# Top-k attention and a leaky-ReLU MLP on one core: first units transposed on TensorE, and the first 256-token chunk begun pair by pair

## The chip, the cores and the metric

The kernel runs on one core of a Trainium2 chip. A core has five engines that work through their own queues in order and meet at semaphores: TensorE (PE in the profile, with PEld for its weight loads), VectorE (DVE), ScalarE (ACT), GpSimd (POOL) and SyncE (SP), which here issues the DMA transfers. PE writes its results into PSUM, eight banks of 2 KB a partition; everything else lies in SBUF or in device memory. The metric is the time of one execution in device microseconds. Five executions of the kernel before took 1484.49, 1484.82, 1487.24, 1488.46 and 1490.54 us: median 1487.24.

## The reference

Attention over 8 batches with 8 heads each, 576 tokens and head size 64, where each query keeps only its 32 largest scores; then an MLP over all 4608 tokens.

```python
scores = scale * np.matmul(q, k.transpose(0, 1, 3, 2))
kth = np.partition(scores, -top_k, axis=-1)[..., -top_k:-top_k + 1]
scores = np.where(scores >= kth, scores, -1000000000.0)
attn = np.exp(scores - np.max(scores, axis=-1, keepdims=True))
attn = attn / (np.sum(attn, axis=-1, keepdims=True) + 1e-09)
attn_out = np.matmul(attn, v)
x = attn_out.transpose(0, 2, 1, 3).reshape(B * S, H * D)     # 4608 x 512
h = x @ w_in                                                 # 512 -> 2048
out = np.maximum(0.01 * h, h) @ w_out                        # 2048 -> 512
```

Everything is in float32.

## The kernel before

**Units.** Heads are taken in pairs, since two heads of 64 fill 128 partitions: 32 pairs, four to a batch (`HP = 4`). A `Unit` is 128 query rows of one pair, both heads; the 64 tokens left over from 576 = 4 x 128 + 64 go two pairs to a unit. A batch is 18 units, the whole kernel 144. In batch 0 the units go through the tokens 0 to 127 for pairs 0 to 3 (units 0 to 3), then 128 to 255 (4 to 7), 256 to 383 (8 to 11), 384 to 511 (12 to 15), and the rest (16, 17).

**A unit's way.** PE computes the scores (L214) into two "wide" PSUM tiles and one "narrow" one, two banks each; ACT copies them to SBUF (L221). DVE finds the 32 largest in four rounds (`top_k`, L244 to L252). POOL subtracts a large number from all others (`mask`, L262, L263). ACT takes the exponent and its sum (L266), adds the small constant (`sums`, giving `ze`, L271); DVE takes the reciprocal (`rz`, L275), ACT multiplies by it (`normalize`, L278). The weights must then be transposed for the product with v. Normally this goes by DMA (`transpose`): ACT splits each 32-bit word into two halves (L287, two copies), SP writes both to device memory (`apart`, L288) and reads them back with a DMA transpose into `wT` (L290). For the units in `HURRIED` PE transposes instead (`transpose_in_haste`, L300: nine 128x128 transposes into two "wide" tiles), and ACT copies the result (`keep_transposed`, L306). Last, PE multiplies v by `wT` for a couple of units (`weigh_values`, L327) and ACT copies the result into the chunk's x (`keep_values`, L341).

**Chunks.** The MLP works on chunks of tokens, two of 128 and then seventeen of 256 (`CHUNKS`). A chunk may begin when all units of all four pairs that hold its tokens have been kept; `ready_at` lists when that is. `mlp(ch)` is a generator that issues a few matmuls at a time: for the first two chunks the first layer in `hidden_of_few` (L352, then transposes L362), for the others L378 with the activation on ACT (L384), then the second layer (L390) and the output (L397, L398). In L378 the four pairs of x are the four terms of one sum in PSUM, in `ps_ml`, which has two banks. `gT` holds the hidden values of one chunk; so chunks go one after the other.

**The order of the work** is written out by hand, the same loop for all engines, and each engine executes its part of it in order. Step s of the loop at the end issues: the top-k of unit s in four slots on DVE; the mask, exponents and sums of unit s - 1; reciprocals, normalization and transposes of unit s - 2; on even s the scores of units s + 2 and s + 3; and at MIDDLE or END of a step the values of the couple of units for which `values_at` gives this place. Between the slots `mlp_steps(budget)` is called seven times. While one of the two first chunks is the latest, or none, the budget of a call is `EARLY_SHARE`; later it is the backlog divided evenly over the slots until the next chunk is ready. At the end of each step `load_more` issues loads of q, k and v of later pairs on SP.

```python
    HURRIED = (15, 23, 31)
    UNHURRIED = 14
        if n < UNHURRIED:
            return (n | 1) + LAG + 1, MIDDLE
        return (n | 1) + LAG - ((n | 1) in HURRIED), END
```

So the values of units 2 and 3 come at the middle of step 7, those of 6 and 7 at the middle of step 11, those of 14 and 15 at the end of step 17. `late` decides whether a unit's reciprocals come after the first slot of a step or after the second (`weights_of`). Before all this, until about 70 us, the weights of the MLP are loaded and put together from double words (`round_weights`).

Of the kernel before, what the change touches and what calls it, by code (L numbers as in the profile page):

```python
# [19 lines left out]
def kernel(  # L20
# [168 lines left out]
    for b in range(B):  # L189
        first = b % 2 == 1  # L190
        whole = [Unit(b, [b * HP + hp], q0 + LEFT * first)
                 for q0 in range(0, S - LEFT, P) for hp in range(HP)]
        left = [Unit(b, [b * HP + hp, b * HP + hp + 1], 0 if first else S - LEFT)
                for hp in range(0, HP, 2)]
        units += left + whole if first else whole + left
# [27 lines left out]
    def first_scores(u):  # L223

        ps = [ps_sc.tile([P, 2, 512], F32, name="wide", bufs=2) for i in range(2)]
        for half in range(2):
            for i, pi, side, r0 in u.parts:
                qt, kt = qk_of[pi]
                d = slice(side * D, (side + 1) * D)
                nc.tensor.matmul(ps[i][:, half, 0:HS], qt[d, u.q0:u.q0 + P],  # L230
                                 kt[d, half * HS:(half + 1) * HS], start=True, stop=True)
        u.both = work.tile([P, 2, S], F32, name="s_sb", bufs=5)
        u.s = [u.both[:, i, :] for i in range(2)]
        for i in range(2):
            nc.scalar.copy(u.s[i].rearrange("p (h n) -> p h n", h=2), ps[i][:, :, 0:HS])
# [129 lines left out]

    def mlp(ch):
# [6 lines left out]
        for f0 in range(0, NFC if ch >= EARLY else 0, 2):  # L373
            ph = ps_ml.tile([P, 2, CHMAX], F32, name="ph", tag="ml")
            for i in range(2):
                f = f0 + i
                for c in range(HP):
                    nc.tensor.matmul(  # L378
                        ph[:, i, 0:n], w_in[c][:, f * P:(f + 1) * P], x[c][:, 0:n],
                        start=(c == 0), stop=(c == HP - 1),  # L380
                    )
                    if c == 1 or i == 0 and c == HP - 1:
                        yield 2 * max(n, 225)
            nc.scalar.activation(gT[:, f0:f0 + 2, 0:n], ph[:, :, 0:n], AF.Prelu, alpha=SLOPE)  # L384
            yield 2 * max(n, 225)
# [24 lines left out]
    def mlp_steps(budget):  # L410
        owed[0] += budget
        while owed[0] > 0:
            if running[0] is None:
                if not ready:
                    owed[0] = 0.0
                    return
                running[0] = mlp(ready.pop(0))
# [11 lines left out]
    HURRIED = (15, 23, 31)  # L429
# [3 lines left out]
    def values_at(n):  # L433

        if n < UNHURRIED:
            return (n | 1) + LAG + 1, MIDDLE
        return (n | 1) + LAG - ((n | 1) in HURRIED), END

# [13 lines left out]
    def attended(*place):  # L452
        for at, ch in ready_at:
            if at == place:
                ready.append(ch)
                backlog[0] += mlp_cost(ch)

# [8 lines left out]
    EARLY_SHARE = 500  # L466
    SLOTS = 7

    with tc.manual_schedule():
        last = {p: n for n, u in enumerate(steps) for p in u.pairs}  # L470

        def load_more(s):

            for of, load, n, lag in ((qk_of, load_qk, LOADED + 3, -2), (v_of, load_v, LOADED_V, LAG + 1)):
                while len(of) < NPAIR and (len(of) < n or last[len(of) - n] + lag <= s):
                    load(len(of))

# [26 lines left out]
        def values(*place):  # L504
# [4 lines left out]
            else:  # L509
                return  # L510
            for part in (weigh_values, keep_values):
                for n, u in enumerate(due):
                    part(u, po[:, n, :])
            attended(*place)

        for s in range(len(steps) + LAG + 1):
# [8 lines left out]

            slot()
# [4 lines left out]
            if older and not late:  # L531
                weights_of(older)
            mlp_steps(budget)
            values(s, MIDDLE)
# [3 lines left out]
            if s - 2 in HURRIED:  # L538
# [4 lines left out]
            if older:  # L543
                keep_transposed(older) if s - 2 in HURRIED else transpose(older)
# [5 lines left out]
            if old:  # L550
                exponents(old, 1)
                sums(old)
            if new and s < HURRY:
                scores(new)
            values(s, END)
# [65 lines left out]
```

## Time and profile before

| what | value |
|---|---|
| median of five executions | 1487.24 us |
| profiled execution, its own time | 1484.49 us |
| its span, first to last instruction | 1482.7 us |
| busy PE / PEld | 1394.8 us (94%) / 928.9 us (63%) |
| busy DVE | 1328.7 us (90%) |
| busy ACT / POOL | 1096.1 us / 1096.0 us (74% each) |
| mean granted PE clock | 0.979 of full speed |
| chain that ended last, by engine | PE 77%, DVE 17%, ACT 3%, DMA 2% |
| L390, second layer, 1152 records | 509.4 us |
| L378, first layer, 2176 records | 481.8 us |
| L327, values, 3200 records | 180.2 us |
| L287, split copies, 282 | 309.1 us, 1144 ns each |
| L300, transposes on PE, 27 | three units |

How to read it: a float32 matmul leaves two records, so 64 records of L378 are 32 matmuls. "Busy" of an engine is an average over the whole span; which engine sets the pace changes between the first 240 us and the rest, and is read from busy times by stretch and from the waits. A row of the view by time gives start, duration, engine, line, operation, tiles, count and in brackets the idle time before it with the instruction that ended it. The wait of an engine that isn't the bottleneck costs nothing by itself, but an engine's queue is in order: what stands behind the waiting instruction is late too.

### The profile page before, as it was taken

How to read it: one execution, taken by the hardware profiler on the slowest of the kernel's cores; microseconds unless marked ns; L12 is line 12 of the kernel's file. 1: busy time of each engine (PE TensorE's matmuls, PEld its weight loads, DVE VectorE, ACT ScalarE, POOL GpSimd, SP SyncE). 2: the span in 40 equal slices, each digit the busy share in tenths (PEclk: the TensorE clock that was granted, in tenths of full speed). 3: DMA queues.
4: the chain of work that ended last, by engine and by line, in shares of the span. 5: the costliest groups of instructions: out<-in, count | busy, mean ns of one | idle time of the engine just before them, and what ended most of it. 6: DMA issues, size and time to landing. Idle time of an engine off the chain costs nothing.

```text
span 1482.7 us, 24084 instructions
## 1 busy us (share of the span) xinstructions
PE 1394.8 (94%) x8059; PEld 928.9 (63%) x8059; DVE 1328.7 (90%) x3414; ACT 1096.1 (74%) x1979; POOL 1096.0 (74%) x742
## 2 busy tenths in 40 slices
PE   6715998999999999999999999999999999999998
PEld 2303546676666766676767666767676767676674
DVE  7999998999999999999999999999999999999600
ACT  8647886877788877787877777777777787877720
POOL 2278887788788887788878888888888888788700
PEclk9967998999999999999999999999999999999999
DMA  8824454635565465655665555556655555654510
GB/s 320 305 63 130 120 164 123 173 111 148 155 167 155 137 167 160 182 140 151 184 163 144 139 167 171 164 142 153 182 161 145 129 142 133 165 131 140 144 47 14
DMA packets 391420, 223.48 MB, mean 151 GB/s; under 512 B 336256, under 2 KB 336256, under 8 KB 389248
## 3 DMA queue, kind: packets, MB, share of 16 engines
q1 hardware_dynamic: 391296, 221.95, 53.6%
q8 instruction: 63, 1.03, 0.3%
q14 instruction: 61, 0.50, 0.1%
HBM read 46.14 MB, written 92.60 MB: 94 GB/s over the span
## 4 chain that ended last, share of the span: by engine, by line
PE 77%; DVE 17%; ACT 3%; DMA 2%; issue 1%; POOL 0%; DVEq 0%; SPq 0%; ACTq 0%
PE pz L390 29%; PE ph L378 28%; PE wide L327 10%; DVE tops L249 6%; PE wide L214 5%; DVE pairs L252 5%; PE narrow L214 3%; DVE pairs L244 2%; PE ph L352 1%; ACT split L287 1%; DMA apart<-split 1%; DVE w_out L149 1%; ACT s_sb L266 1%; ACT s_sb L278 1%; DVE w_in L149 1%
## 5 line engine op out<-in xcount | busy, mean ns | idle before, releaser
L262 POOL TENSOR_SCALAR pen<-s_sb,tops 128x576 f32<-128x576 f32 x288 | 637.4, 2213 | 217.3 <-DVE tops L249 126.2
L249 DVE MAX8 tops<-pairs 128x8 f32<-128x288 f32 (+1 forms) x1152 | 636.8, 593 | 0.0
L390 PE MATMUL pz<-w_out,gT 128*128 128x512 f32 x1152 | 509.4, 597 | 0.0
L378 PE MATMUL ph<-x,w_in 128*128 128x256 f32 x2176 | 481.8, 381 | 0.0
L252 DVE MATCH_REPLACE8 pairs<-tops,pairs 128x288 f32<-128x288 f32 (+1 forms) x864 | 460.8, 539 | 0.0
L378 PEld LDWEIGHTS ph<-x,w_in 128*128 128x128 f32 x2176 | 411.3, 190 | 77.4 <-issue 23.1
L263 POOL TENSOR_TENSOR s_sb<-s_sb,pen 128x576 f32<-128x576 f32 x288 | 406.1, 1410 | 24.1
L390 PEld LDWEIGHTS pz<-w_out,gT 128*128 128x128 f32 x1152 | 215.9, 190 | 266.3 <-issue 264.9
L287 ACT COPY split<-s_sb 128x1152 uint16<-128x1152 uint16 x282 | 309.1, 1144 | 0.0
L278 ACT ACTIVATE s_sb<-s_sb,rz 128x576 f32<-128x576 f32 x288 | 207.0, 769 | 35.3 <-DVE rz L275 35.3
L266 ACT ACTIVATE s_sb<-s_sb,nbias 128x576 f32<-128x576 f32 x288 | 220.9, 767 | 12.7 <-POOL s_sb L263 12.7
L244 DVE TENSOR_TENSOR pairs<-s_sb 128x576 f32<-128x576 f32 x288 | 213.6, 780 | 9.9
L327 PE MATMUL wide<-wT,vt 128*64 128x128 f32 (+1 forms) x3200 | 180.2, 269 | 32.6 <-ACT s_sb L221 25.0
L327 PEld LDWEIGHTS wide<-wT,vt 128*64 128x64 f32 x3200 | 162.8, 140 | 75.0 <-ACT s_sb L221 29.6
L384 ACT ACTIVATE gT<-ph 128x512 f32<-128x512 f32 x136 | 80.6, 593 | 80.8 <-PE ph L378 80.8
L341 ACT COPY x<-wide 128x128 f32<-128x128 f32 (+1 forms) x160 | 32.2, 260 | 145.7 <-PE wide L327 145.6
L221 ACT COPY s_sb<-wide 128x704 f32<-128x704 f32 x142 | 107.1, 754 | 21.1 <-PE wide L214 21.1
L214 PE MATMUL wide<-kt,qt 64*128 64x352 f32 (+1 forms) x392 | 74.7, 491 | 24.3 <-ACT s_sb L221 23.6
L275 DVE RECIPROCAL rz<-ze 128x2 f32<-128x2 f32 x144 | 22.6, 157 | 52.5 <-ACT ze L271 52.4
L221 ACT COPY s_sb<-narrow 128x448 f32<-128x448 f32 x142 | 68.7, 536 | 0.6
L397 ACT COPY o_sb<-pz 128x512 f32<-128x512 f32 x36 | 21.1, 586 | 58.4 <-PE pz L390 58.4
L252 DVE MATCH_VALUE_LOAD pairs<-tops,pairs 128x8 f32 x864 | 63.7, 74 | 0.0
(62 smaller groups left out, 622.8 us busy)
## 6 DMA issues: line engine op xcount, KB each, us to landing
apart<-split SPq DMA_DIRECT2D x282, 288.0 KB, 2.1
raw<-in_weights_dram SPq DMA_DIRECT2D x16, 1024.0 KB, 6.5
vt<-in_vk_dram SPq DMA_DIRECT2D x32, 320.0 KB, 3.5
out_dram<-o_sb SPq DMA_DIRECT2D x36, 256.0 KB, 2.0
qt<-in_qT_dram SPq DMA_DIRECT2D x20, 288.0 KB, 4.1
kt<-in_kT_dram SPq DMA_DIRECT2D x20, 288.0 KB, 4.6
raw<-in_qT_dram SPq DMA_DIRECT2D x12, 288.0 KB, 3.1
raw<-in_kT_dram SPq DMA_DIRECT2D x12, 288.0 KB, 3.5
```

The lines of the kernel that those rows point to most:

```text
L214: nc.tensor.matmul(to[r0:r0 + u.rows, i, :], qt[d, u.q0:u.q0 + u.rows], kt[d, k0:k1], start=True, stop=True)
L244: nc.vector.tensor_tensor(pairs[:, :, n, :], u.both[:, :, 0:HS], u.both[:, :, HS:S], op)
L249: nc.vector.max(out=u.tops[:, i, r, :], in_=rest[i])
L252: nc.vector.match_replace(out=rest[i], in_to_replace=u.tops[:, i, r, :], in_values=rest[i], imm_value=LOWEST)
L262: nc.gpsimd.tensor_scalar(pen, u.s[i], u.tops[:, i, ROUNDS - 1, 7:8], MASKED, ALU.is_lt, ALU.mult)
L263: nc.gpsimd.tensor_tensor(u.s[i], u.s[i], pen, ALU.add)
L266: nc.scalar.activation(u.s[i], u.s[i], AF.Exp, bias=u.nbias[:, i:i + 1], scale=SCALE, accum_out=u.z[:, i:i + 1])
L278: nc.scalar.activation(u.s[i], u.s[i], AF.Copy, bias=0.0, scale=u.rz[:, i:i + 1])
L287: nc.scalar.copy(split, pairs[:, :, h])
L327: nc.tensor.matmul(po[side * D:(side + 1) * D, o, :], vt[:, c, side, :], u.wT[:, c + side * NKC if c + 1 < NKC else c, r:r + n], start=(c ...
L378: nc.tensor.matmul(ph[:, i, 0:n], w_in[c][:, f * P:(f + 1) * P], x[c][:, 0:n], start=(c == 0), stop=(c == HP - 1),)
L390: nc.tensor.matmul(pz[0:m, 0:DMODEL], gT[:, f, r0:r0 + m], w_out[f // 4][:, f % 4, :], start=(f == 0), stop=(f == NFC - 1),)
```

## The change

- In batch 0 the last two groups of 128 tokens are taken pair by pair: units 8 and 9 are both of pair 0, 10 and 11 of pair 1, 12 and 13 of pair 2, 14 and 15 of pair 3.
- Units 0, 1, 2, 3, 7 and 14 are transposed on PE too (`HASTY`); 3 and 7 count as hurried, so that the values of 2 and 3 come at the end of step 5, and those of 6 and 7 at the end of step 9. In the step after next to a hurried unit, before step 20, its reciprocals and normalization come first of all.
- `begin_hidden` sums half of chunk 2's first layer (8 of 16 column blocks) over the pairs 0 and 1 when the values of unit 11 are kept, and over pair 2 when those of unit 13 are, into four PSUM banks: the "narrow" tile and both of `ps_ml`. `mlp(2)` then adds pair 3.
- The copies of x after values in the middle of a step go to the end of the step, unless a chunk becomes ready there or a hurried unit is two steps back.
- The scores of units 18 and 19 use `first_scores` (only "wide" tiles), since "narrow" is taken.
- `load_more` issues v ahead of q and k, and q and k of a pair 8 steps after the last unit that used the buffer (2 steps before it until now), one pair a step.
- `EARLY_SHARE` is 510 instead of 500.

```diff
+        tiles = [(0,), (P,), (2 * P, 3 * P)] if b == 0 else [(q0,) for q0 in range(0, S - LEFT, P)]
         whole = [Unit(b, [b * HP + hp], q0 + LEFT * first)
-                 for q0 in range(0, S - LEFT, P) for hp in range(HP)]
+                 for q0s in tiles for hp in range(HP) for q0 in q0s]
...
+    def begin_hidden(ch, pairs):
+        n = CHUNKS[ch]
+        x = x_of[ch]
+        if ch not in begun:
+            first = ps_sc.tile([P, 2, 512], F32, name="narrow").rearrange("p h (f n) -> p h f n", n=CHMAX)
+            begun[ch] = [first[:, 0], first[:, 1]]
+            begun[ch] += [ps_ml.tile([P, 2, CHMAX], F32, name="ph", tag="ml") for k in range(2)]
+        done = 0
+        for f in range(NFC // 2):
+            for c in pairs:
+                nc.tensor.matmul(begun[ch][f // 2][:, f % 2, 0:n], w_in[c][:, f * P:(f + 1) * P], x[c][:, 0:n],
+                                 start=(c == 0 and f % 2 == 0), stop=False)
+                done += 1
+                if done % 2 == 0:
+                    yield 2 * n
...
-            ph = ps_ml.tile([P, 2, CHMAX], F32, name="ph", tag="ml")
+            first = 0
+            if ch in begun and f0 < NFC // 2:
+                ph, first = begun[ch][f0 // 2], HP - 1
+            else:
+                ph = ps_ml.tile([P, 2, CHMAX], F32, name="ph", tag="ml")
             for i in range(2):
                 f = f0 + i
-                for c in range(HP):
+                for c in range(first, HP):
...
-    HURRIED = (15, 23, 31)
+    HURRIED = (3, 7, 15, 23, 31)
+    HASTY = (0, 1, 2, 3, 7, 14, 15, 23, 31)
...
-        if n < UNHURRIED:
-            return (n | 1) + LAG + 1, MIDDLE
-        return (n | 1) + LAG - ((n | 1) in HURRIED), END
+        if (n | 1) in HURRIED:
+            return (n | 1) + LAG - 1, END
+        return ((n | 1) + LAG + 1, MIDDLE) if n < UNHURRIED else ((n | 1) + LAG, END)
...
     def attended(*place):
         for at, ch in ready_at:
             if at == place:
-                ready.append(ch)
+                ready.append(mlp(ch))
                 backlog[0] += mlp_cost(ch)
+        for last, pairs in ((11, (0, 1)), (13, (2,))):
+            if values_at(last) == place:
+                ready.append(begin_hidden(EARLY, pairs))
...
-    EARLY_SHARE = 500
+    EARLY_SHARE = 510
...
-            for of, load, n, lag in ((qk_of, load_qk, LOADED + 3, -2), (v_of, load_v, LOADED_V, LAG + 1)):
+            for of, load, n, lag in ((v_of, load_v, LOADED_V, LAG + 1), (qk_of, load_qk, LOADED + 3, 8)):
                 while len(of) < NPAIR and (len(of) < n or last[len(of) - n] + lag <= s):
                     load(len(of))
+                    if lag > LAG + 1 and len(of) > n:
+                        break
...
+            at_first = s < HURRY and s - 2 in HURRIED
+            if at_first:
+                weights_of(older)
             slot()
...
-            if older and not late:
+            if older and not late and not at_first:
                 weights_of(older)
             mlp_steps(budget)
-            values(s, MIDDLE)
+            weighed = values(s, MIDDLE)
+            at_once = s - 2 in HURRIED or any(at == (s, MIDDLE) for at, _ in ready_at)
+            if at_once:
+                keep(weighed, s, MIDDLE)
             slot()
             if older and late:
                 weights_of(older)
-            if s - 2 in HURRIED:
+            if s - 2 in HASTY:
                 transpose_in_haste(older)
...
             if old:
                 exponents(old, 1)
                 sums(old)
+            if not at_once:
+                keep(weighed, s, MIDDLE)
             if new and s < HURRY:
-                scores(new)
-            values(s, END)
+                if s == 16:
+                    first_scores(new[0])
+                    first_scores(new[1])
+                else:
+                    scores(new)
+            keep(values(s, END), s, END)
```

`values` now only issues the matmuls and returns what is to be kept; `keep` issues the copies of x and calls `attended`. `first_scores` takes units of fewer rows too.

## The prediction

> **What bounds the kernel now.** I read the page's 40 slices first, then busy time by stage, then TensorE's waits, then the reciprocals on VectorE, because each answer says which engine to ask next.
>
> ```profile
> PE   6715998999999999999999999999999999999998
> DVE  7999998999999999999999999999999999999600
> ...
> PEclk9967998999999999999999999999999999999999
> ```
> A slice is 37 us. TensorE (PE) is full from about slice 7 to the end, VectorE (DVE) until slice 37. TensorE has free time only early, and its clock is low there.
>
> ```profile
> 74.00:137.00 63.00, 14.45 (x114) 11.36 (x112) 62.48 (x163) 35.05 (x64) 50.66 (x33) 0.62 0.34 91
> 137.00:240.50 103.50, 91.13 (x524) 50.19 (x522) 98.24 (x257) 78.84 (x149) 83.41 (x56) 0.94 0.51 145
> 240.50:1482.70 1242.20, 1236.48 (x7251) 844.88 (x7250) 1107.19 (x2882) 928.55 (x1711) 942.72 (x631) 1.00 0.53 145
> ```
> Each row gives a stretch, its length, then busy time of PE, PEld, DVE, ACT, POOL. From 240.5 us, where chunk 2's first layer begins, PE idles 5.7 us in 1242. So either chunk 2 begins earlier, or PE has less left by then, or nothing is won. The changed kernel does some of both.
>
> ```profile
> PE wide L327 <- ACT s_sb L221: 25.0, 2, 13.5
> PE wide L214 <- ACT s_sb L221: 23.6, 1, 23.6
> PE wide L327 <- DMA wT<-apart: 5.6, 1, 5.6
> ```
> (TensorE's waits from 74 to 300 us: total, times, longest.) The first two lie before 137 us: nothing is ready. The last is unit 14's transposed weights, late by DMA.
>
> But DVE is no spectator. One unit's top-k starts (L244) every 8.86 us (404.18 to 537.11 in 15 steps), while PE needs 73.8 us for eight units and a chunk (first-layer stretches begin at 692.00 and 765.79 in the chain of waits), 9.22 a unit. DVE could be only 0.36 us a unit faster, and it has lost time:
>
> ```profile
> 219.05 0.17 DVE L275 RECIPROCAL rz<-ze 128x2 f32<-128x2 f32 x1 [3.35 <-ACT ze L271]
> 251.25 0.17 DVE L275 RECIPROCAL rz<-ze 128x2 f32<-128x2 f32 x1 [3.94 <-ACT ze L271]
> 260.49 0.17 DVE L275 RECIPROCAL rz<-ze 128x2 f32<-128x2 f32 x1 [1.86 <-ACT ze L271]
> 398.25 0.17 DVE L275 RECIPROCAL rz<-ze 128x2 f32<-128x2 f32 x1 [2.81 <-ACT ze L271]
> ```
> All its waits are of this kind: 14.6 us by step 36, 10.6 of them before step 25. The cause is ScalarE's queue standing at a copy of x that waits for PE:
>
> ```profile
> 213.40 0.43 ACT L341 COPY x<-wide 128x128 f32<-128x128 f32 x2 [4.33 <-PE wide L327]
> 240.55 0.43 ACT L341 COPY x<-wide 128x128 f32<-128x128 f32 x2 [7.49 <-PE wide L327]
> ```
> And by steps 36 to 44 attention is just in time for PE:
>
> ```profile
> 412.60 1.31 PE L327 MATMUL wide<-wT,vt 128*64 128x128 f32 x20 [0.70 <-DMA wT<-apart]
> ```
> Unit 35's transpose was issued at 424.10 and takes 4.6 us, and PE uses it at 429.12; unit 39's was issued at 458.18 and is used at 462.50. So the end can move forward only as far as the smaller of two gains: PE's at chunk 3, and DVE's by step 36 to 44. After that PE's 0.36 us a unit restores slack.
>
> **The change, part by part.**
>
> *Hasty units 0, 1, 2, 3, 7, 14.* Before, a unit's way from normalized weights to wT is two splits on ACT (2.19 us), two transfers (2.1 landing, 6.27 at unit 14), a DMA transpose (4.6): 9 to 13 us. Unit 15's row of the same profile gives the new way: nine PE transposes 1.43 us, two copies on ACT 1.17. ACT saves 1.0 us a unit. PE pays 6 x 1.43 = 8.6 us, but units 0 to 3 lie in the stretch with 14.45 of 63 us busy, so only 7 and 14 count: 2.9 us. In the cold stretch forty value matmuls took 4.12 us at 115.58 and 2.33 later, so a transpose there may cost 1.43 to 2.5; I take 2.5 early, where it delays only what follows at once.
> The Trainium skill (TensorE: Matmul & The Clock Gate, Part 1) says that the array runs at half clock until about 3.4 us of sustained work, which speaks against short transposes between idle gaps; the granted 0.62 agrees. By the rule each early transpose costs 2.9 us and the start below comes 0.4 us later than I have it.
>
> *Values of units 2, 3 at step 5's end, not step 7's middle.* Step 5 starts at 113.7. Unit 3's ze is there by then (114.69 before, with 2.2 us of splits ahead of it that go). In ACT's order the copies of the scores for units 6 and 7 (2.5 us) come first: normalize to about 117. PE first runs the values of 0, 1 (cold, 4 us), then unit 3's transposes to about 121.5; copies to 122.8; values of 2, 3 (cold, 3.8) to 126.6; copy of x 0.4. The first layer of chunk 0 starts at 127 instead of 137.0: 10 us. Lower bound of the gain 5 (the two "wide" PSUM buffers are now shared with transposes and may make each other wait), upper 13 (clock warm).
>
> *What PE then has to do until chunk 2 is complete.* Chunk 0 and 1: first layer 29.3 us, transposes of it 5.5, second layer 27.8 (64 records at 0.435): 62.6. Values of six couples of units, 2.33 each: 14.0. Six score pairs at 2.2: 13. Transposes of 7, 14, 15: 4.3. New ahead of its turn: half of chunk 2's first layer for three pairs, 8 x 3 = 24 matmuls, 0.438 each by the 14.01 us for 64 records (two records a matmul): 10.5. Sum 104.4, plus idle time: before, PE lost 6.3 us from 137 to 226 waiting for ACT inside hidden_of_few, which stays; I add 2 for the PSUM buffers. 127 + 104.4 + 8 = 239.5, against 240.5 now. So chunk 2 is complete only 1 us earlier, but with 10.5 us of it done: PE gains 11.5.
>
> *Four PSUM banks held (narrow, both ml) from step 15 to 18.* Unit 18 and 19's scores use "wide" four times over two buffers: each waits for a copy of 0.65 us, at most 2.6 us; PE has other work behind it in order, so I count 1 within the 2 above.
> The Trainium skill (Perfetto Trace Analysis, Optimizing Tensor Performance) advises rotating matmul groups through different banks so that evacuation overlaps; holding four banks goes against it. The wide waits above, 25.0 and 23.6 us, show that PE does stop for such buffers, though there nothing else was ready. By the rule the four uses expose the whole 2.6 us.
>
> *Chunk 2's remainder.* 56 - 10.5 + 17.9 (values and scores of eight units) + 1.4 = 64.9: PE would be at chunk 3 at 304.4 rather than 316.7. Attention allows it at step 25 plus 10.7 (reciprocal at +3.0, normalize, transposes, copies, values, x, by unit 23's rows). Step 25 without DVE waits is 69.6 + 25 x 8.86 = 291.1 (302.3 now).
>
> *DVE's waits.* The step 16 and 19 waits (3.35 and 3.94) lose their cause: x is kept at the step's end, behind ze, and unit 14 no longer waits for DMA. But PE is later against the program in steps 12 to 17 (scores of 16, 17 at 127 + 31.3 + 17.4 + 10.4 of the two chunks + 8.8 scores + 7 values + 1.4 + 6.3 idle = 209.6 instead of 205.2, needed at 211.4 plus delays), and at steps 5, 9 and 17 the reciprocal now stands in front of the unit's whole top-k. There ze has about 0.8 us of slack (mask 7.4 us, exponent and sums 0.9, step 8.9). I take 3.5 us of waits before step 25 instead of 10.6, bounds 0 and 11. Chunk 3 then starts at 305.3: gain 11.4.
> After step 25 the program is the old one with PE as late against DVE as before; of the 4.0 us of waits in steps 28 to 35 I keep 2.5.
>
> *q, k loads later, one pair a step.* Eight issues at 209 to 224 us go from in front of unit 14's and 15's transfers. They return at steps 24 to 27, and pairs 12 to 15 at steps 40 to 43, where attention has no slack. Four loads right ahead of a transfer made its transpose issue 6.8 us later instead of 3.2 (224.54 against 216.99); one pair 2.7 us ahead made no difference (393.01, 395.70, 398.93). Between 0 and 3.6 I take 0.5. The v loads keep their steps.
>
> *Order of units 8 to 15, EARLY_SHARE 510:* the same instructions, the share 2% up; nothing on the path.
>
> **Sum.** PE's gain 11.4. DVE's gain 14.6 - 3.5 - 2.5 = 8.6, less 0.5: 8.1; where ACT is freer a few tenths come back. The smaller decides: 8.5 us. The profiled execution took 1484.49 us (span 1482.7), so 1476; it was the lowest of five with median 1487.24, so the median to expect is 1478.7, say 1478.5.
>
> **The rivals.**
> 1. *DVE loses almost nothing* (1472): all 14.6 us go and PE starts near 124. For it: deferred x copies take away the only releaser in DVE's list. Against it: PE does not get faster in steps 8 to 17.
> 2. *The waits only move* (1485): PE, carrying 10.5 us more before step 17, holds scores and ACT back, DVE loses some 10 us before step 25 again, and attention, tight at step 36, gives PE's gain back as waits for wT. Gain 14.6 - 10 - 2.5 = 2. Here also falls a start of chunk 0 at 132 or later.
> 3. *Slower: the reciprocal at a step's head* (1491). In step 9 ze of unit 8 came at 163.3, 14.1 us after the step's start, where 8.0 would do: ACT stood behind hidden_of_few. With 0.8 us of slack the same delay stops DVE's next top-k for 5.3 us; at steps 5, 9 and 17 that is 16, plus the 2.5 left: 18.5 against 14.6, 4 us slower. It decides from about 4 us a time on. Against it: the first MLP work starts only after step 5's reciprocal, and begun sums in step 16 need no ACT.
>
> **How the numbers follow.** Forecast (1475 to 1482) 0.52, rival 1 0.14, rival 2 0.21, rival 3 0.13. The range must leave out at most 0.2: 1469 to 1487 leaves rival 3 and a small tail of rival 1 out; the forecast's own is 1475 to 1482. Under 0.3% (4.5 us, about what a measurement here tells from none) counts as the same: faster is the forecast, rival 1 and a third of rival 2, 0.73; same 0.14; slower 0.13.
>
> **What would show it.** The first matmuls of hidden_of_few near 127 us (right) or after 132 (wrong); the first matmul of chunk 2's last pair near 239; DVE's L244 of step 25 near 295 and of step 36 near 396; no copy of x holding ACT for over 4 us between 200 and 245; PE waits for wT of 2 to 4 us between 385 and 470. The prediction is wrong if DVE waits before step 25 exceed 8 us, or if steps 5, 9, 17 begin with a reciprocal that waits.

## The result: 0.2% faster, and the waits have only moved

The changed kernel takes 1483.82 us (median of 33 executions, 1480.90 to 1488.32) against 1487.01 us for the kernel before (55 executions): a ratio of 0.9979, 95% interval 0.9974 to 0.9985. That is 3.2 us, where 8.5 us were forecast and where 0.3% (4.5 us) had been set as the least that counts as faster. Its profiled execution took 1483.44 us, with a span of 1481.7 us against 1482.7.

The 40 slices of the changed kernel's page (37 us each, busy tenths):

```profile
PE   6728989999999999999999999999999999999999
...
DVE  7999988999999999999999999999999999999600
...
PEclk9958999999999999999999999999999999999999
```

TensorE stands at 2 and 8 in the third and fourth slice, where it stood at 1 and 5; but in the sixth both TensorE and VectorE have gone from 9 to 8. The busy times by stretch of the same kernel (PE, PEld, DVE, ACT, POOL) say the same in us:

```profile
74.00:137.00 63.00, 35.38 (x196) 23.31 (x196) 62.52 (x164) 35.35 (x72) 51.84 (x34) 0.67 0.05 15
137.00:240.50 103.50, 92.28 (x547) 54.28 (x549) 96.00 (x250) 73.67 (x142) 81.38 (x55) 0.97 0.36 100
240.50:1482.70 1242.20, 1229.72 (x7214) 836.67 (x7210) 1109.11 (x2887) 929.41 (x1711) 944.92 (x632) 1.00 0.54 146
```

TensorE does 21 us more in the first row, as meant. But VectorE does 2.2 us less between 137 and 240.5, and TensorE, which idled 5.7 us in the last stretch before, now idles 11.5 (the row's 12.5 has 1.0 us after the end of the span). TensorE's work by time shows where (start, duration, line, tiles, count; in brackets the idle time before it and what ended it). The kernel before, at chunk 2:

```profile
235.98 4.54 PE L327 MATMUL wide<-wT,vt 128*64 128x128 f32 x40 [5.60 <-DMA wT<-apart]
240.44 5.77 PE L378 MATMUL ph<-x,w_in 128*128 128x256 f32 x22
```

The changed kernel, whose lines have other numbers (L354 is L352 of before, L382 is `begin_hidden`, L404 is L378, L343 is L341; the experiments shift some by one or two):

```profile
122.76 7.13 PE L354 MATMUL ph<-w_in,x 128*128 128x512 f32 x16
...
218.64 4.11 PE L382 MATMUL narrow<-x,w_in 128*128 128x256 f32 x10 [4.43 <-ACT x L343]
...
241.65 1.13 PE L404 MATMUL narrow<-x,w_in 128*128 128x256 f32 x4 [0.53 <-ACT x L343]
...
299.68 1.31 PE L329 MATMUL wide<-wT,vt 128*64 128x128 f32 x20 [2.23 <-DMA wT<-apart]
...
315.14 3.07 PE L404 MATMUL ph<-x,w_in 128*128 128x256 f32 x13
```

The first MLP work starts at 122.76 us, 14.3 us earlier than before (137.03). Chunk 2's last pair starts at 241.65, 1.2 us later than chunk 2 began before, with half of the first layer for three pairs behind it. Then TensorE waits for attention (2.23 us and smaller ones before 315), and chunk 3 begins at 315.1 instead of 316.6. So 14.3 us in front have become 1.4.

Why attention is no earlier stands in VectorE's reciprocals that waited, by time:

```profile
218.30 0.17 DVE L277 RECIPROCAL rz<-ze 128x2 f32<-128x2 f32 x1 [3.51 <-ACT ze L273]
225.88 0.17 DVE L277 RECIPROCAL rz<-ze 128x2 f32<-128x2 f32 x1 [1.75 <-ACT ze L273]
251.79 0.17 DVE L277 RECIPROCAL rz<-ze 128x2 f32<-128x2 f32 x1 [2.39 <-ACT ze L273]
260.10 0.17 DVE L277 RECIPROCAL rz<-ze 128x2 f32<-128x2 f32 x1 [0.93 <-ACT ze L273]
...
396.70 0.17 DVE L277 RECIPROCAL rz<-ze 128x2 f32<-128x2 f32 x1 [2.27 <-ACT ze L273]
```

The first four are 8.6 us; with 1.4 us before step 16 that makes 10.0 us ahead of step 25, where the kernel before had 10.6. The second stands at the head of step 17, and so does one of 0.67 us at the head of step 9. ScalarE's queue by time shows what stood ahead of the first of these `ze`:

```profile
208.58 1.46 ACT L280 ACTIVATE s_sb<-s_sb,rz 128x576 f32<-128x576 f32 x2
213.82 0.59 ACT L423 COPY o_sb<-pz 128x512 f32<-128x512 f32 x1 [3.77 <-PE pz L416]
214.30 0.78 ACT L268 ACTIVATE s_sb<-s_sb,nbias 128x576 f32<-128x576 f32 x1
...
215.07 2.19 ACT L289 COPY split<-s_sb 128x1152 uint16<-128x1152 uint16 x2
217.16 0.78 ACT L268 ACTIVATE s_sb<-s_sb,nbias 128x576 f32<-128x576 f32 x1
...
218.06 0.20 ACT L273 ACTIVATE ze<-z 128x2 f32<-128x2 f32 x1
218.17 0.41 ACT L343 COPY x<-wide 128x128 f32<-128x128 f32 x2
```

The copy of x is behind `ze`, as the change wants. But the copy of chunk 1's output is ahead of it, and it waits 3.77 us for the second layer's last sum. At the same place before, the copy of x waited 4.33 us. By these waits TensorE was some 4 us late against the program there in both kernels; only the instruction that stands and waits is another one. And since x now comes last, at 218.17, TensorE's begun sums wait 4.43 us for it. From the beginning of the MLP to 260 us ScalarE's waits for TensorE tell the same. In the kernel before (137 to 260 us) they sum to 29.5 us, 20.6 of them at copies of x; in the changed one (122 to 260 us) to 37.2 us, 11.4 of them at copies of x and the rest at `scale` (6.4), scores (5.1 and 3.8), outputs (4.5), transposes (3.0) and `gT` (3.0).

### The profile page after: what moved, and what is told of

The parts are those of the page before. It is cut to its first block, busy times and chain, and to the rows that moved or that the text cites. A ratio compares the mean times of both kernels' runs of the same rounds, so it can differ in the third digit from the quotient of the medians.

```text
span 1481.7 us, 24181 instructions
## 1 busy us (share of the span) xinstructions
PE 1407.1 (95%) x8113; PEld 935.0 (63%) x8113; DVE 1329.6 (90%) x3414; ACT 1092.1 (74%) x1979; POOL 1097.3 (74%) x742
## 3 DMA queue, kind: packets, MB, share of 16 engines
q8 instruction: 64, 1.05, 0.3%
## 4 chain that ended last, share of the span: by engine, by line
PE 78%; DVE 13%; ACT 5%; DMA 3%; issue 1%; SPq 0%; POOL 0%; DVEq 0%; ACTq 0%
PE pz L416 31%; PE ph L404 26%; PE wide L329 10%; PE wide L216 5%; DVE tops L251 5%; DVE pairs L254 4%; PE narrow L216 3%; ACT split L289 2%; DMA wT<-apart 1%; DVE pairs L246 1%; ACT s_sb L280 1%; ACT s_sb L268 1%; DMA apart<-split 1%; DVE w_out L149 1%; DVE w_in L149 1%
## 5 line engine op out<-in xcount | busy, mean ns | idle before, releaser
L404 PE MATMUL ph<-x,w_in 128*128 128x256 f32 x2120 | 469.4, 381 | 0.0
L404 PEld LDWEIGHTS ph<-x,w_in 128*128 128x128 f32 x2120 | 399.9, 190 | 75.7 <-issue 22.9
L289 ACT COPY split<-s_sb 128x1152 uint16<-128x1152 uint16 x270 | 295.9, 1145 | 0.0
L268 ACT ACTIVATE s_sb<-s_sb,nbias 128x576 f32<-128x576 f32 x288 | 221.2, 768 | 12.5 <-POOL s_sb L265 12.5
L329 PEld LDWEIGHTS wide<-wT,vt 128*64 128x64 f32 x3200 | 158.7, 137 | 50.0 <-ACT ze L273 17.4
L329 PE MATMUL wide<-wT,vt 128*64 128x128 f32 (+1 forms) x3200 | 177.2, 266 | 7.6 <-DMA wT<-apart 6.0
L343 ACT COPY x<-wide 128x128 f32<-128x128 f32 (+1 forms) x160 | 32.2, 260 | 133.6 <-PE wide L329 133.5
```

The lines of the kernel that those rows point to most:

```text
L268: nc.scalar.activation(u.s[i], u.s[i], AF.Exp, bias=u.nbias[:, i:i + 1], scale=SCALE, accum_out=u.z[:, i:i + 1])
L289: nc.scalar.copy(split, pairs[:, :, h])
L329: nc.tensor.matmul(po[side * D:(side + 1) * D, o, :], vt[:, c, side, :], u.wT[:, c + side * NKC if c + 1 < NKC else c, r:r + n], start=(c ...
L404: nc.tensor.matmul(ph[:, i, 0:n], w_in[c][:, f * P:(f + 1) * P], x[c][:, 0:n], start=(c == 0), stop=(c == HP - 1 and (i == 1 or not first)),)
```

## The experiments

Each was measured beside the kernel before, whose medians in the four groups were 1487.38 (e1 to e4), 1487.49 (e5 to e8, the same chip), 1487.16 (e9 to e12, a second chip) and 1488.81 us (e13 to e15, a third). A ratio is against the kernel before of the same group, so kernels of different groups are best compared by their ratios. Most have 5 to 12 executions, e9 has four. "Waits" are VectorE's waits for `ze` in the profiled execution, by steps; the last column is the start of chunk 3's first layer.

| run | median | ratio, 95% interval | waits before 16 / 16 to 24 / 25 to 35 | chunk 3 |
|---|---|---|---|---|
| before | 1487.01 | 1 | 1.1 / 9.6 / 4.0 | 316.6 |
| after | 1483.82 | 0.9979 [0.9974, 0.9985] | 1.4 / 8.6 / 3.4 | 315.1 |
| e1 | 1483.74 | 0.9977 [0.9968, 0.9986] | 1.3 / 14.3 / 8.8 | 316.3 |
| e2 | 1487.45 | 1.0002 [0.9991, 1.0013] | 1.4 / 13.3 / 10.0 | 315.3 |
| e3 | 1481.25 | 0.9963 [0.9949, 0.9977] | 1.5 / 5.2 / 5.1 | 311.8 |
| e4 | 1483.67 | 0.9979 [0.9969, 0.9989] | 1.5 / 9.5 / 3.9 | 316.6 |
| e5 | 1478.73 | 0.9937 [0.9923, 0.9952] | 1.5 / 4.3 / 3.3 | 310.3 |
| e6 | 1478.05 | 0.9934 [0.9920, 0.9947] | 1.5 / 0.0 / 5.3 | 305.3 |
| e7 | 1482.71 | 0.9965 [0.9953, 0.9978] | 1.4 / 10.1 / 1.4 | 314.3 |
| e8 | 1480.35 | 0.9947 [0.9933, 0.9960] | 4.9 / 1.8 / 2.7 | 309.6 |
| e9 | 1472.62 | 0.9910 [0.9895, 0.9926] | 1.4 / 0.0 / 2.7 | 304.3 |
| e10 | 1485.56 | 0.9993 [0.9983, 1.0002] | 5.1 / 6.3 / 4.9 | 317.1 |
| e11 | 1476.48 | 0.9932 [0.9920, 0.9945] | 0.0 / 3.6 / 3.8 | 308.2 |
| e12 | 1479.98 | 0.9955 [0.9943, 0.9968] | 1.3 / 4.2 / 3.8 | 310.6 |
| e13 | 1480.81 | 0.9947 [0.9934, 0.9961] | 0.2 / 3.1 / 3.8 | 308.9 |
| e14 | 1485.14 | 0.9978 [0.9969, 0.9987] | 1.2 / 7.8 / 5.5 | 314.7 |
| e15 | 1482.25 | 0.9956 [0.9943, 0.9968] | 5.4 / 3.7 / 3.5 | 314.3 |

One reading holds over the table: from chunk 3 to the end of the span it is 1166 to 1171 us in all 17 profiles. So what makes chunk 3 earlier makes the kernel shorter, to within 5 us; a smaller difference than that can't be read from this column alone.

**Is it VectorE's own pace?** If so, less work on VectorE brings the end forward. e1 and e2 take one round of the four from one head in steps 18 to 31, in the changed kernel and in the one before.

```diff
-            for i in range(2):
+            for i in range(2 - (u.short and r == ROUNDS - 1)):
                 nc.vector.max(out=u.tops[:, i, r, :], in_=rest[i])
             if r + 1 < ROUNDS:
-                for i in range(2):
+                for i in range(2 - (u.short and r == ROUNDS - 2)):
...
+    for u in steps[18:32]:
+        u.short = True
```

> The changed kernel, but for units 18 to 31 VectorE leaves out the fourth round of the second head (one match-replace and one max of 576, 0.73 + 0.67 us); that head's threshold is the 24th largest instead of the 32nd. VectorE then gets up to 14 x 1.0 us ahead (GpSimd's 7.8 us a unit limits it). Theory A, attention sets the time: what TensorE gained at chunk 2 is given back as waits for wT between 240 and 470 us (6 us of idle there), so the time falls by 4 to 7 us against the changed kernel, and TensorE's waits for wT there nearly vanish. Rival B, TensorE sets it and its gain was never there: within 1.5 us of the changed kernel.

> The kernel before, with the same rounds left out. Theory A: TensorE has no idle time to win there (1.9 us of waits after 240 us), so the gain is 0 to 2 us against the kernel before, less than half of what the same edit brings to the changed kernel. Rival B: the same small gain in both. Rival C, VectorE sets the time in both kernels: 4 us or more in both.

Both gave nothing: e1's theory A, 4 to 7 us, missed. VectorE's busy time fell by 10.9 us in e1 (1329.6 to 1318.7), and all of it came back as waiting. The list of VectorE's waits from 140 to 420 us (total, times, longest) has one line for e1, where the changed kernel has 13.4 us in 9:

```profile
DVE rz L278 <- ACT ze L274: 24.4, 13, 3.7
```

VectorE's own work, then, does not set the pace there: what it waits for came no earlier when it was ahead. TensorE is the busier engine from chunk 3 on, 104.5 of the 105 us from 315 to 420 us in e1. The edit begins at step 18, so it says nothing about the waits at steps 16 and 17.

**Does the begun half layer pay, and do the loads?** e3 takes `begin_hidden` out of the changed kernel (and with it the special scores of units 18 and 19); e4 puts the loads of q and k back to their old steps.

```diff
-            if values_at(last) == place:
+            if False:
                 ready.append(begin_hidden(EARLY, pairs))
...
-                if s == 16:
+                if False:
```

> The changed kernel without begin_hidden: chunk 2's first layer is summed over all four pairs when it is complete, and units 18 and 19 take their scores as other units do. Theory A: the 10.5 us of sums ahead bought little, because TensorE waited afterwards; without them TensorE is less late against VectorE in steps 15 to 17, VectorE's waits there shrink from 5.3 to about 2 us, and the time is within 3 us of the changed kernel, either way. Rival B: the sums ahead are a real gain of TensorE, and the time rises by 6 to 10 us.

```diff
-            for of, load, n, lag in ((v_of, load_v, LOADED_V, LAG + 1), (qk_of, load_qk, LOADED + 3, 8)):
+            for of, load, n, lag in ((v_of, load_v, LOADED_V, LAG + 1), (qk_of, load_qk, LOADED + 3, -2)):
```

> The changed kernel with q and k loaded as early as before (2 steps before the last use of the buffer rather than 8 after), still one pair a step at most. Theory A: the loads of pairs 12 to 15 leave steps 40 to 43, where unit 39's halves took 3.5 us to land instead of 2.1 and TensorE waited 0.7 us for its wT: 1 to 2 us faster. If the loads' new place is free or helps: the same or 1 us slower.

Without the begun sums the kernel is no slower; its median is 2.6 us lower, though the two intervals touch. Chunk 2 begins at 235.7 us with nothing done, and step 25 comes 3.5 us earlier than in the changed kernel (297.9 against 301.4), although the wait in step 16 has grown to 5.17 us (3.51 in the changed kernel): those of 1.75, 2.39 and 0.93 us behind it are gone, and it is between them that the begun sums ran. The loads are worth nothing in either place: e4's 1 to 2 us missed.

**Is it the place of ScalarE's waiting instruction?** e5 moves a single instruction and its DMA: chunk 1's output copy goes behind the unit's `ze`.

```diff
-            nc.scalar.copy(o_sb[0:m], pz[0:m, 0:DMODEL])
-            nc.sync.dma_start(out[t0 + r0:t0 + r0 + m, :], o_sb[0:m])
+            def put(o_sb=o_sb, pz=pz, m=m, r0=r0):
+                nc.scalar.copy(o_sb[0:m], pz[0:m, 0:DMODEL])
+                nc.sync.dma_start(out[t0 + r0:t0 + r0 + m, :], o_sb[0:m])
+            if ch == 1:
+                puts.append(put)
+            else:
+                put()
...
                 sums(old)
+            while puts:
+                puts.pop()()
```

> The changed kernel with one instruction moved in ScalarE's order: chunk 1's output copy, which stands ahead of unit 14's exponents and unit 13's splits in step 15 and waits 3.8 us there for TensorE, comes after ze of unit 14. Theory A2 (ScalarE's order sets attention: what waits for TensorE holds ze and the splits back): VectorE's wait of 3.5 us in step 16 and TensorE's of 4.4 us for x in front of the first begun sums both nearly go, step 25 comes 3 to 5 us earlier, and the time falls by 2 to 5 us against the changed kernel. Rival B (TensorE's own work sets the time): within 1 us, the wait turning up elsewhere.

It gained 5.1 us (1483.82 to 1478.73; the intervals are apart). ScalarE's queue of e5 at the place shown above:

```profile
209.36 1.46 ACT L280 ACTIVATE s_sb<-s_sb,rz 128x576 f32<-128x576 f32 x2
210.70 0.78 ACT L268 ACTIVATE s_sb<-s_sb,nbias 128x576 f32<-128x576 f32 x1
...
214.46 0.20 ACT L273 ACTIVATE ze<-z 128x2 f32<-128x2 f32 x1
214.59 0.58 ACT L424 COPY o_sb<-pz 128x512 f32<-128x512 f32 x1
215.07 0.44 ACT L343 COPY x<-wide 128x128 f32<-128x128 f32 x2
```

Nothing here waits for TensorE any more: `ze` comes at 214.46 instead of 218.06 although the normalization before it ran 0.8 us later (step 0 began 0.7 us later), the reciprocal's 3.51 us is gone, and x, now at 215.07, costs TensorE 0.58 us instead of 4.43, as TensorE's rows of e5 show:

```profile
215.57 2.43 PE L382 MATMUL narrow<-x,w_in 128*128 128x256 f32 x10 [0.58 <-ACT x L343]
```

That shows the cause of these two waits by an edit that touches little else: one copy that waits for TensorE, ahead of a `ze` that VectorE needs. Its 5.1 us are nearly all of the 5.3 us that the change fell short of its forecast. They hold for this order of the work only: with another share (e10, below) the same move gains nothing.

**What are the begun sums worth once that is gone?** e6 is e5 without them; e9 is e5 with half as many: four column blocks in the two `ps_ml` banks, "narrow" left free, and units 18 and 19 scored as usual.

```diff
-            first = ps_sc.tile([P, 2, 512], F32, name="narrow").rearrange("p h (f n) -> p h f n", n=CHMAX)
-            begun[ch] = [first[:, 0], first[:, 1]]
-            begun[ch] += [ps_ml.tile([P, 2, CHMAX], F32, name="ph", tag="ml") for k in range(2)]
+            begun[ch] = [ps_ml.tile([P, 2, CHMAX], F32, name="ph", tag="ml") for k in range(2)]
...
-        for f in range(NFC // 2):
+        for f in range(NFC // 4):
...
-            if ch in begun and f0 < NFC // 2:
+            if ch in begun and f0 < NFC // 4:
```

> The changed kernel without begin_hidden and with the same copy moved. Theory A2: VectorE's wait of 5.2 us in step 16 goes, but TensorE, which idled only 2.6 us between 240 and 480 us without the begun sums, has little left to win there: 1 to 4 us faster than without begin_hidden alone (1481.25). Rival B: within 1 us of it. If the two edits are worth the same with and without begun sums, the begun sums themselves are a loss of about 2.5 us at any rate.

> The changed kernel with chunk 1's output copy moved behind ze of unit 14, and with only a quarter of chunk 2's first layer summed ahead (4 column blocks, 12 matmuls, 5.3 us, in the two ml banks), so that units 18 and 19 take their scores into the narrow tile as other units do. Theory A2: in steps 15 to 19 ScalarE waits less for TensorE than with half of the layer, VectorE's wait of 3.4 us in step 19 shrinks, and TensorE keeps some of the 5.3 us: 1476 to 1478.5. Rival: sums ahead are worth nothing in any amount, since chunk 2 completes as much later: 1478 to 1479.

Half a layer ahead is worth nothing: e6 without it equals e5 with it (0.9934 and 0.9937). A quarter makes e9 the best kernel of all: 1472.62 us, 14.5 us below the median before of its group (ratio 0.991), better than the 1476 to 1478.5 expected. Over e5 that is 6.1 us by the medians, but about 4 us by the ratios, whose intervals touch. Its waiting reciprocals up to step 35, by time:

```profile
148.52 0.17 DVE L277 RECIPROCAL rz<-ze 128x2 f32<-128x2 f32 x1 [0.66 <-ACT ze L273]
...
180.18 0.17 DVE L277 RECIPROCAL rz<-ze 128x2 f32<-128x2 f32 x1 [0.49 <-ACT ze L273]
...
198.43 0.17 DVE L277 RECIPROCAL rz<-ze 128x2 f32<-128x2 f32 x1 [0.23 <-ACT ze L273]
...
385.76 0.17 DVE L277 RECIPROCAL rz<-ze 128x2 f32<-128x2 f32 x1 [2.67 <-ACT ze L273]
```

and the beginning of chunk 2's last pair and of chunk 3:

```profile
229.31 2.95 PE L402 MATMUL ph<-x,w_in 128*128 128x256 f32 x12 [0.53 <-ACT x L343]
...
304.31 5.34 PE L402 MATMUL ph<-x,w_in 128*128 128x256 f32 x24
```

Chunk 2 starts at 229.3 us in e9 and at 229.7 in e6, but in e9 a quarter of its layer for three pairs is done, while e5, with the half, starts it only at 236.9. The quarter fits into what TensorE had free, in two ways. From 200 to 229 us TensorE idles 3.9 us in e6 and 0.9 in e9. And its mean granted clock in that stretch is 0.88 in e6 and 1.00 in e9: after 1.94 us of idle time the nine transposes of unit 14 take 2.12 us in e6, without it 1.15 in e9. So some 3.0 of the quarter's 5.3 us came from less idle time and the rest from other work that ran faster. From 229 to 304 us TensorE is busy all 75.0 us in e6 and 71.2 us in e9. So e6 stands at TensorE's limit and e9 has 3.8 us of slack there; attention has no waits left in steps 16 to 24 in either. Step 25 comes at 291.3 us in e9, where the prediction had 291.1 without any wait, so little is left to win ahead of chunk 3. The 2.6 us by which e6's VectorE waits more from step 25 to 35 agree with the difference at chunk 4 (382.1 against 379.3).

**The other edits of the change.** e7 leaves the reciprocals of hurried units where they were; e8 gives the early MLP a smaller share; e10 joins e5's edit with a share between the two; e15 keeps x in the middle of a step as before.

```diff
e7   -            at_first = s < HURRY and s - 2 in HURRIED
     +            at_first = False
e8   -    EARLY_SHARE = 510
     +    EARLY_SHARE = 470
e10  -    EARLY_SHARE = 510
     +    EARLY_SHARE = 480
e15  -            at_once = s - 2 in HURRIED or any(at == (s, MIDDLE) for at, _ in ready_at)
     +            at_once = True
```

> The changed kernel with the reciprocals and the normalization of units 3, 7 and 15 after the first slot, as for other units next to a hurried one. Rival 3 of the prediction (a reciprocal at a step's head stops VectorE): its waits of 0.7 and 1.75 us at steps 9 and 17 go, 1 to 2 us faster. Theory A2: these two are small beside the ones that ScalarE causes, and units 3, 7 and 15 come 2 to 3 us later to TensorE: 0 to 3 us slower, above all since chunk 2 waits for unit 15.

> The changed kernel with EARLY_SHARE 470 instead of 510: TensorE gets 8% less MLP work a step before chunk 2 is ready, is less late against the others, and has more to do after it, where it idles 7.7 us now. Theory A2: ScalarE waits less for TensorE in steps 8 to 17, VectorE's waits before step 25 fall from 10 to about 6 us, 1 to 4 us faster. Rival B: work that isn't done early is missing later, 2 to 5 us slower.

> The changed kernel with the same copy moved and EARLY_SHARE 480. Theory A2: TensorE's lateness in steps 8 to 17 and the moved copy cure the same wait in step 16, so the two don't add: 1477 to 1479, against 1478.73 with the copy alone. If they add (5.1 + 3.4 us): 1475 or less.

> The changed kernel with all copies of x directly after their values again. Theory A2: in steps 13 and 15 ScalarE then waits for the values of units 8 to 11 in front of exponents and ze, while in the changed kernel the output copy of chunk 1 stands there anyway: 1 to 6 us slower than the changed kernel. If the later copies are worth as much as alone: 10 us slower.

e7 gained about 1 us, not beyond its interval: one wait grew to 5.30 us as others went. e8 gained 3.5 us with one number: the waits before step 16 rise from 1.4 to 4.9 us, those of steps 16 to 24 fall from 8.6 to 1.8. e15, expected slower, gained too (0.9956 against 0.9979), in the same way: 5.4 and 3.7. There ScalarE stands 3.42 us at a copy of x at 197.86 us and 3.20 us at the next one at 214.71; chunk 1's output copy, behind them at 216.61, waits no more, and TensorE's begun sums no longer wait for x. e10 missed: two edits of a kind that gain 5.1 and 3.5 us alone left the kernel at 0.9993, no faster than the changed kernel and hardly faster than the one before. Two of its reciprocals before step 20:

```profile
151.60 0.17 DVE L277 RECIPROCAL rz<-ze 128x2 f32<-128x2 f32 x1 [3.33 <-ACT ze L273]
...
252.51 0.17 DVE L277 RECIPROCAL rz<-ze 128x2 f32<-128x2 f32 x1 [4.35 <-ACT ze L273]
```

The wait at 218 us has gone and two others have grown: 3.33 us at step 9 (0.67 in the changed kernel), where the reciprocal stands at the step's head, and 4.35 us at step 19 (2.39). By this reading the share decides which MLP instruction lies ahead of which `ze`, and so where TensorE's lateness is paid. The share 480 was not run without the moved copy, and why it hits a worse place than 470 was not traced.

**Parts of the change on the kernel before.** e11 adds to the kernel before only that copies of x in the middle of a step go behind `ze`; e12 only the six units transposed on TensorE; e13 both.

```diff
e11  +        kept = []
     ...
     -            for part in (weigh_values, keep_values):
     -                for n, u in enumerate(due):
     -                    part(u, po[:, n, :])
     -            attended(*place)
     +            for n, u in enumerate(due):
     +                weigh_values(u, po[:, n, :])
     +            def keep():
     +                for n, u in enumerate(due):
     +                    keep_values(u, po[:, n, :])
     +                attended(*place)
     +            if place[1] == END or any(at == place for at, _ in ready_at):
     +                keep()
     +            else:
     +                kept.append(keep)
     ...
                      sums(old)
     +            while kept:
     +                kept.pop()()
e12  +    HASTY = (0, 1, 2, 3, 7, 14, 15, 23, 31)
     ...
     -            if s - 2 in HURRIED:
     +            if s - 2 in HASTY:
                      transpose_in_haste(older)
     ...
     -                keep_transposed(older) if s - 2 in HURRIED else transpose(older)
     +                keep_transposed(older) if s - 2 in HASTY else transpose(older)
```

> The kernel before, with one part of the change alone: copies of x after values in the middle of a step go to its end, behind ze, unless a chunk becomes ready there. Theory A2: the wait of VectorE in step 16 (3.35 us, behind the copy of x of units 10 and 11) goes, the one in step 19 (behind TensorE's wait for unit 14's wT) stays: 1 to 3 us faster than before. If TensorE alone set the time: within 1 us.

> The kernel before, with units 0, 1, 2, 3, 7 and 14 transposed on TensorE and nothing else (the values keep their places). TensorE's wait of 5.6 us for unit 14's wT and most of VectorE's 3.9 us in step 19 go; the transposes of 7 and 14 cost 2.9 us of TensorE: 2 to 5 us faster than before by theory A2. If the gain needs the earlier places of the values too: within 1.5 us.

> The kernel before with the later copies of x and the six hasty units, and nothing else of the change. If the two cure different waits (the copies step 16's and ScalarE's behind values, the hasty units TensorE's wait for unit 14's wT and step 19's): 1472 to 1475. If they cure the same lateness, which is spent by step 25: 1475.5 to 1477, as with the copies alone.

Both misses upwards: e11 alone gained 10.7 us, more than three times what the whole change did, and e12 alone 7.2 us. Together they gave 0.9947, no more than e11 alone (0.9932) and not clearly more than e12 alone (0.9955); its 1480.81 us lie above both ranges expected. ScalarE's queue of e11 where the kernel before waited 4.33 us for x:

```profile
212.53 0.20 ACT L271 ACTIVATE ze<-z 128x2 f32<-128x2 f32 x1
212.63 0.42 ACT L341 COPY x<-wide 128x128 f32<-128x128 f32 x2
```

`ze` is early and x is not late either: TensorE's lateness now passes while ScalarE does other work. In the kernel before, chunk 1's output copy comes later (at 226.57 us, without a wait), so x was the only copy at that place that waits, and moving it ended the loss; in the changed kernel, whose MLP starts 14.3 us earlier, the output copy had taken its place. TensorE's wait for unit 14's weights is gone from e11 as well:

```profile
232.85 7.17 PE L378 MATMUL ph<-x,w_in 128*128 128x256 f32 x32
```

Chunk 2 begins 7.6 us earlier, although unit 14 still goes by DMA. Its two halves took about as long as before (6.3 us instead of 6.8 from the first write's issue to the transpose's), but ScalarE split it at 215.65 instead of 221.35 us, and its DMA transpose was issued at 224.93 instead of 231.31. So that wait of 5.60 us, which the prediction put down to DMA and cured by a hasty unit, came in good part from the same copy of x. This fits that the hasty units add nothing to e11.

Last, e14 takes the earlier places of the values of units 2, 3, 6 and 7 from e3, and with them the early reciprocals of units 3 and 7: `HURRIED = (15, 23, 31)`.

> The changed kernel without begun sums and with the values of units 2, 3, 6, 7 at their old places (HURRIED 15, 23, 31), hasty units, later copies, order of units, loads and EARLY_SHARE 510 as changed. If the earlier places with their reciprocals ahead of the top-k and their TensorE work running into step 15 take the gain: 1473 to 1477, 4 us or more below 1481.25 of the changed kernel without begun sums. If they help: 1482 to 1486, since chunk 0 starts 14 us later.

It gave 0.9978 against e3's 0.9963, with overlapping intervals, and a step 25 that is 3.3 us later (231.6 against 228.3 us after step 0). So the earlier start helps a little or not at all; it isn't what takes the gain.

## Why the prediction was wrong, step by step

- *First MLP work at 127 us*: 122.76. The gain was 14.3 us, over the upper bound of 13. The work just ahead was quicker than taken: values of units 0 and 1 3.28 us (4 taken), transposes of unit 3 1.20 (2.5), values of 2 and 3 2.40 (3.8).
- *Chunk 2's last pair at 239.5 with 10.5 us of sums done*: 241.65. From its start TensorE took 118.9 us, not 104.4 + 8: 106.6 us of work and 12.3 us of idle time. The work is 2.2 us over its sum; the idle time is 4.3 us over the 8 taken (its own terms, 6.3 and 2, give 8.3), and one wait of 4.43 us, for an x that now comes behind `ze`, is as large as that. The change's own cure of one wait had made another, and the working had priced the late copy at nothing.
- *Chunk 2's remainder, 64.9 us*: 73.5 us from 241.65 to 315.14, of which TensorE worked 68.1 and idled 5.4.
- ***VectorE's waits before step 25, "I take 3.5 us instead of 10.6"*: 10.0. This is the step that failed.** It reasoned that the waits of steps 16 and 19 "lose their cause" when the copy of x moves and unit 14 no longer goes by DMA. They stayed: 3.51 us in step 16 instead of 3.35, 2.39 in step 19 instead of 3.94, and 1.75 us at the head of step 17 came in addition. The copy of x was the place, not the cause. The cause is that TensorE runs some 4 us behind the program at step 15, and the next instruction on ScalarE that needs TensorE ahead of a `ze` inherits that: here chunk 1's output copy. For step 16 e5 shows it by moving that copy, e11 by moving x where no other copy followed. For step 19 no edit touches the place alone; ScalarE stands 3.65 us at a copy of x at 241.16 us there, 7.49 before. Its sign of being wrong came true in both halves: more than 8 us of waits before step 25, and waiting reciprocals at the heads of steps 9 and 17 (0.67 and 1.75 us). The working saw that TensorE would be late ("PE is later against the program in steps 12 to 17") but didn't look which of ScalarE's instructions would then stand at that place.
- *Chunk 3 at step 25 plus 10.7 us*: 13.7 (301.4 to 315.1). In the kernel before it was 14.2 (302.3 to 316.6), which the trace had shown: the 10.7 was built from rows of one unit; what it left out was not traced. A second error of 3 us in the same direction.
- *Steps 28 to 35, 2.5 us of waits kept*: 2.27, and 1.14 more in step 26.
- *Attention is what the end follows, with step 36 near 396*: the mechanism fits. Step 36 came at 402.6 instead of 404.2; from there to the end of the span it is 1078.5 to 1082.1 us in all 17 profiles, and in 13 of them chunk 3 begins 13.0 to 14.2 us after step 25 (in the other four 11.5 to 15.5). The sum "14.6 - waits before 25 - waits after" with the measured 10.0 and 3.4 gives 1.2 us; the spans differ by 1.0.
- *Loads of q and k, 0.5 us*: nothing that e4 could tell.
- *Four PSUM banks held, 1 us*: the scores of units 18 and 19 waited 0.74 us, and chunk 2's remainder 0.69. The Trainium skill (Perfetto Trace Analysis, Optimizing Tensor Performance) advises rotating groups through different banks; e9, which holds two instead of four, has a ratio of 0.9910 against e5's 0.9937, but it also sums less ahead, so the runs do not show how much of that is the banks.
- *TensorE waits for `wT` of 2 to 4 us between 385 and 470*: 1.2. With attention hardly earlier there was little of TensorE's gain to give back there; it was given back before 315, where TensorE was busy 68.6 of 74.5 us between 240.5 and 315.

Rival 2, "the waits only move", is what happened, with nearly its numbers: some 10 us of waits again before step 25, and a gain of 2 us by its sum. Its other half was off: TensorE's gain went before chunk 3, with waits for `wT` of 1.92 us at 265 and 2.23 us at 300 us, not at step 36. Rival 3 had a true mechanism that needed another alignment: e10 shows 3.33 us at the head of step 9, near its point of 4 us.

One thing made the small gain look smaller in the profiles: the execution profiled before was the lowest of its first five, the one after an ordinary one. By medians the gain is 3.2 us, by profiles 1.05.

## What to carry to other kernels

When an in-order engine waits at a copy for a late producer, name how late the producer is and list every instruction on that engine that needs it ahead of the urgent one; moving only the first of them hands the wait to the second. Edits that each cure the same lateness need not add (e11, e12 and e13; e10 even lost what e5 had gained), so try them singly: here one part alone gained three times as much as the whole. A wait that the profile puts down to a DMA may begin with the engine that fed it. And work done ahead paid here only as far as it fitted into free time: a quarter of the layer did, a half did not.

## What was not expected of the hardware

- Kernels differ in how steady they are. Five executions of e11 lay within 0.9 us and five of e12 within 0.7 us, while the 15 of the kernel before in the same group spread over 5.5 us. In the profiles, one execution of each kernel, the time from the first layer of chunk 7 (at 605 to 618 us) to the end lies between 864.6 and 868.4 us, though all do the same work there. The cause is open.
- In the changed kernel nine transposes took 2.18 us when TensorE had been mostly idle (after 20.49 us of idle time at 91.57 us, but after only 1.59 us at 100.44 as well; the mean granted clock from 92 to 116 us is 0.50) and 1.20 us at 118.15, when TensorE had worked without a pause since 110.80. The Trainium skill (TensorE: Matmul & The Clock Gate, Part 1) has half the clock until some 3.4 us of sustained work; by that, as an estimate, the cold ones would take 2.4 us, a little more than the trace shows.
